# Squares and normalisation on GpSimd, omega scaled once, and block 0's gate work in two pieces

## The chip, the cores and the metric

One core of a Trainium2 chip. The metric is device time in microseconds, the median of three timed runs. The core has five engines that run side by side, each through its own queue in order: PE (TensorE, matrix products), DVE (VectorE), ACT (ScalarE), POOL (GpSimd) and SP, which here issues DMAs. They wait for each other through semaphores.

## The reference

A linear-attention layer with random features, followed by a gated feed-forward layer.

```python
scale = 1.0 / np.sqrt(np.sqrt(D))
def phi(x):                                   # x is q * scale or k * scale
    proj = np.einsum('bhsd,md->bhsm', x, omega)
    sq = np.sum(x * x, axis=-1, keepdims=True) / 2.0
    h = proj - sq
    h = h - np.max(h, axis=-1, keepdims=True)
    return np.exp(h) / np.sqrt(m)
kv = np.einsum('bhsm,bhsd->bhmd', k_p, v)
z = np.sum(k_p, axis=2)
num = np.einsum('bhsm,bhmd->bhsd', q_p, kv)
den = np.einsum('bhsm,bhm->bhs', q_p, z)[..., None] + 1e-06
x = num / den                                 # heads side by side: 4608 x 512
xn = x / np.sqrt(np.mean(x * x, axis=-1, keepdims=True) + 1e-06) * rms_g
g = xn @ w_gate
out = (g * (1.0 / (1.0 + np.exp(-g))) * (xn @ w_val)) @ w_out
```

8 batches of 8 heads, 576 tokens, head size 64, 128 features; 4608 tokens of 512 columns; an inner width of 1536. The weights of the second layer are 64-bit numbers, which the kernel narrows to 32 bits itself.

## The kernel before

The 4608 tokens are 36 chunks of 128, and 9 blocks of 4 chunks (512 tokens). Three stages follow each other on PE.

The first stage (to about 445 us) makes the attention, and a part of the gated layer with it. For each chunk of k and of q, `features` (L457) loads the chunk (`load`, L465), squares it (`square` on ACT, L472), sums the squares by head (`norm` on DVE, L512, or `norm_pe` on PE for the "lean" chunks, which are the first four of k), projects it on omega (`project` on PE, L521, tiles `pjk` and `pjq`), takes the row's largest value (`peak` on DVE, L536), works out the shift (`shift` on DVE, L542: two operations on 128x8, tiles `hm` and `bi`) and takes the exponentials (`exps` on ACT, L552). `kv_mid` and `kv_half` multiply k's features with v. `attend` (L681) then turns q's features around (`turn`, tiles `qt`, `qpT`), multiplies them with kv (`mix`, tile `nu`), divides on DVE (`divide`, L710, tile `x`), and normalises: `power` on ACT (L725) gives the sum of squares `ss`, `root` on POOL (L732) the inverse root, `scale` on DVE (L739) multiplies x by `ss` and by `g_sb` (rms_g on all partitions). `xturn` turns the chunk around on PE (tile `xt`), `xout` and `xhi` on ACT and `xlo` on POOL (L770) write it as a high and a low part, since every product of the gated layer is made of three passes (`three_pass`, L216): high by high, high by low, low by high.

`gated` (L814) makes 4 of the 12 column groups f of the gated layer during this stage: for block `blk` and group f it runs 12 products of 128x512 for the gate (tile `ff`) and 12 for the value, then `gate` on ACT, `silu` and `value` on DVE, and a store. It needs the four chunks of its block (`xs`, L871) and the narrowed weights of its group (`weights`, L315: ACT takes the size, DVE runs four operations, `mag` twice and `w` twice; ACT and POOL write the high and low parts).

The second stage makes the other 8 column groups, and the third the output product, both by a seven-product scheme on halves; neither is touched.

The order of all this is not the order of the code. Every piece of work is an item with an engine, a duration, what it needs, what buffers it takes, and a key (`Plan.add`, L129). `Plan.order` (L133) plays the items through with these durations and, on each engine, starts the ready item with the smallest key; the instructions are then written out in that order, so each engine's queue is fixed. The table `KEYS` (L37) holds the keys of the first nine chunks and of the weights. While PE has nothing ready and no gated item has begun, the player puts `spin` products in PE's queue (L886): 128x512 products whose result nobody uses. `SWITCH` (L109) is what the player adds when PE goes from one form of product to another.

Of the kernel before, what the change touches and what calls it, by code (L numbers as in the profile page):

```python
# [19 lines left out]
DM = H * D  # L20
DFF = 1536
P = 128
# [14 lines left out]
KEYS = {  # L37
    "k": [-34.2, -24.4, -20.3, -13.7, -13.0, -5.6, -2.0, -0.5, -0.4],
    "q": [-32.4, -12.2, -8.0, -2.2, 3.5, 4.9, 5.3, 6.0, 7.6],
    "w": [  # L40
        -9.6, -3.4, 8.7, 11.5, 8.0, 3.2, 4.4, 5.9,
        -16.1, -0.3, -12.6, -18.6, -20.2, -13.8, 26.9, 39.6,
    ],
    "lead": 4.04,
    "v": 3.37,
    "kv": -15.15,
    "attend": -21.79,
}
AHEAD = 28
PACE = (-2, 2, 0, 1.25)  # L50
FIRST = {"k": 1, "q": 0}
# [6 lines left out]
    "mix": {  # L58
        "xr": (2, 1), "xn": (1, 1), "x": (1, 1), "qpT": (1, 1), "kv": (4, 1), "small": (16, 1),
        "mag": (2, 1), "w": (4, 1), "sr": (1, 1), "f64": (2, 1),  # L60
# [47 lines left out]
FRONT = 0.45  # L108
SWITCH = 0.096  # L109
FILL = 900.0  # L110
# [117 lines left out]
def performer_glu_kernel(  # L228
# [69 lines left out]
    nc.scalar.dma_start(om[D:P, :], omT)  # L298
    heads2 = cpool.tile([P, 4], F32, name="heads2")
    cpool.tile([P, 14], F32, name="pad")  # L300
    nc.gpsimd.memset(heads2, 0.0)
    for i in range(2):
        nc.gpsimd.memset(heads2[i * D : (i + 1) * D, i : i + 1], 1.0 / SCALE)
        nc.gpsimd.memset(heads2[i * D : (i + 1) * D, 2 + i : 3 + i], 1.0)

# [151 lines left out]
    def features(tag, c, key):  # L457
# [14 lines left out]
        def square():  # L472
            n = t["raw"][:, 1, :]
            nc.scalar.activation(n, t["raw"][:, 0, :] if lean else n, AF.Square, scale=0.25)

        def norm_pe():
            t["sq"] = tile_("psM", [P, H], f"sq{nm}")
            for hp in range(4):
                nc.tensor.matmul(
                    t["sq"][:, 2 * hp : 2 * hp + 2],  # L480
                    lhsT=t["raw"][:, 1, hp * P : (hp + 1) * P],
                    rhs=heads2[:, 0:2] if first else heads2[:, 2:4],
                    start=True,
                    stop=True,
                )
# [20 lines left out]
        def exp_half(i):  # L506
            if i == 0:
                st[tag + "p", c] = tile_(tag + "p", [P, H, M], f"{tag}p{c}")
            to = st[tag + "p", c].rearrange("p (a b) m -> p b a m", b=2)
            nc.scalar.activation(to[:, i], t["pts"][i], AF.Exp, scale=SCALE)  # L510

# [30 lines left out]
        def shift():  # L542
            hm = small("hm", f"hm{nm}")
            t["bi"] = small("bi", f"bi{nm}")
            ve.scalar_tensor_tensor(
                out=hm, in0=t["mx"], scalar=SCALE, in1=t["sq"], op0=ALU.mult, op1=ALU.subtract
            )
            ve.scalar_tensor_tensor(  # L548
                out=t["bi"], in0=hm, scalar=-1.0, in1=t["sq"], op0=ALU.mult, op1=ALU.subtract
            )  # L550

        def exps(n):  # L552
            if n == 0:
                st[tag + "p", c] = tile_(tag + "p", [P, H, M], f"{tag}p{c}")
            h0 = n // 2 + 4 * (n % 2)
            for h in (h0, h0 + 2):
                nc.scalar.activation(  # L557
                    st[tag + "p", c][:, h, :],
                    t["pts"][h % 2][:, h // 2, :],
                    AF.Exp,  # L560
                    bias=t["bi"][:, h : h + 1],
                    scale=SCALE,
                )
# [117 lines left out]
    def attend(c, key):  # L681
# [43 lines left out]
        def power():  # L725
            t["xn"] = tile_("xn", [P, DM], f"xn{c}")
            t["ss"] = small("ss", f"ss{c}", 1)
            nc.scalar.activation(  # L728
                t["xn"], t["x"].rearrange("p h d -> p (h d)"), AF.Square, accum_out=t["ss"]
            )  # L730
# [8 lines left out]
        def scale():  # L739
            ve.scalar_tensor_tensor(  # L740
                out=t["xn"],
                in0=t["x"].rearrange("p h d -> p (h d)"),
                scalar=t["ss"],
                in1=g_sb,
                op0=ALU.mult,
                op1=ALU.mult,
            )

# [40 lines left out]
        for half in range(2):  # L789
# [23 lines left out]

    def gated(blk, f, key):  # L814
        t = {}

        def ff(j, a=0, z=TB, only=None):
            xhi, xlo = st["xT", blk]
            if a == 0 and not only:
                t[j] = tile_(bank, [P, TB], f"ff{blk}_{f}_{j}")  # L820
            three_pass(
# [10 lines left out]
        def gate():  # L832
            t["t"] = tile_("t", [P, TB], f"t{blk}_{f}")
            nc.scalar.activation(t["t"], t[0], AF.Tanh, scale=0.5)

        def silu():
            t["u"] = tile_("u", [P, TB], f"u{blk}_{f}")
            ve.scalar_tensor_tensor(
# [3 lines left out]
        def value():  # L842
            t["h"] = tile_("h", [P, TB], f"h{blk}_{f}")
            ve.scalar_tensor_tensor(
# [3 lines left out]
        def store():  # L848
            nc.sync.dma_start(h_d[:, f, blk * TB : (blk + 1) * TB], t["h"])
# [5 lines left out]
        at = (blk, f)  # L855
        ws = [[st["w", f, j]] + st.get("ff", []) for j in range(2)]
        give = [("xT", blk)] if f == last else []
        end = blk == NBLK - 1
# [17 lines left out]
        else:  # L876
            g = add("PE", 2.73, lambda: ff(0), xs + ws[0], key, [(bank, at, 0)])
            v = add("PE", 2.73, lambda: ff(1), [g] + ws[1], key, [(bank, at, 1)], give)
        gates.append(v)
        st["ff"] = [v]  # L880
        i = add("ACT", 0.53, gate, [g], top, [("t", at)])
        i = add("DVE", 0.62, silu, [i], top, [("u", at)], [("t", at), (bank, at, 0)])
        i = add("DVE", 0.62, value, [i, v], top, [("h", at)], [("u", at), (bank, at, 1)])
        st["hs", f, blk * TB, TB] = add("SP", 0.26 / RATE, store, [i], top, give=[("h", at)], land=LAND)

# [624 lines left out]
```

## Time and profile before

| | us |
|---|---|
| median of three runs | 1064.76 (1064.54 to 1065.6) |
| span of the profiled execution | 1061.9 |
| busy in it: PE / DVE / ACT / POOL | 1049.1 / 825.5 / 647.7 / 143.8 |
| first gate product starts at | 70.2 |

The profile is of one execution, by the hardware profiler; the span goes from its first to its last instruction, and the page gives no other time of that execution. The runs' times hold what lies around the span as well. A matmul's duration in the trace overlaps the next one's, since they are pipelined, so the pace of PE is read from start to start. "L222" is line 222 of the kernel; a row such as `L474 ACT ACTIVATE inq<-inq ... x36 | 24.8, 695` is a group of 36 instructions with 24.8 us busy in all and 695 ns in the mean; what follows is the engine's idle time before them and who ended it. The granted clock of PE is full throughout.

### The profile page before, as it was taken

The numbers are of one execution on the slowest core, as the hardware profiler recorded it, in microseconds if no ns is written. First come the engines' busy times: TensorE is split into PE (matmuls) and PEld (weight loads), VectorE is DVE, ScalarE is ACT, GpSimd is POOL, SyncE is SP. The second block draws the span as 40 slices with busy tenths as digits, with TensorE's granted clock in tenths as the row PEclk, the third lists the DMA queues.
The fourth block names the chain that finished last, engine by engine and source line by source line (L and its number), as shares of the span: only waits on it lengthen the run. The fifth ranks groups of instructions, "written<-read, shape, count | busy, mean of one in ns | idle before, by whom it ended". The sixth has DMA issues, their size and how long they took to land.

```text
span 1061.9 us, 20636 instructions
## 1 busy us (share of the span) xinstructions
PE 1049.1 (99%) x7755; PEld 881.8 (83%) x7755; DVE 825.5 (78%) x1438; ACT 647.7 (61%) x1428; POOL 143.8 (14%) x185
## 2 busy tenths in 40 slices
PE   9999999999999999999999999999999999999998
PEld 6788888888888888878889788988888888888888
DVE  5989999888887865589889936758649996859573
ACT  7899788868786754556545546535555554444433
POOL 0242221121121221380000324000000000000000
PEclk9999999999999999999999999999999999999999
DMA  7786778566654433776466524434273936172321
GB/s 263 257 267 196 222 246 251 167 212 216 222 178 161 131 134 106 233 245 211 159 188 215 178 81 153 149 104 139 72 266 112 300 131 221 54 217 86 119 91 50
DMA packets 106596, 185.87 MB, mean 175 GB/s; under 512 B 9088, under 2 KB 51456, under 8 KB 106496
## 3 DMA queue, kind: packets, MB, share of 16 engines
q1 hardware_dynamic: 106272, 184.26, 53.7%
q8 instruction: 61, 1.00, 0.4%
q10 hardware_dynamic: 224, 0.30, 0.1%
q14 instruction: 39, 0.32, 0.1%
HBM read 124.49 MB, written 60.03 MB: 174 GB/s over the span
## 4 chain that ended last, share of the span: by engine, by line
PE 82%; DVE 12%; issue 2%; DMA 2%; ACT 1%; SPq 0%; DVEq 0%; ACTq 0%
PE ff L222 6%; PE ff L224 5%; PE ff L223 5%; PE qa L224 5%; PE qa L222 5%; PE qa L223 5%; PE pa L222 4%; PE pa L224 4%; PE pa L223 4%; PE nu L702 3%; PE pjk L527 3%; PE pjq L527 3%; PE kvp L658 3%; PE qt L691 3%; PE qb L224 2%
## 5 line engine op out<-in xcount | busy, mean ns | idle before, releaser
L222 PE MATMUL ff<-xhi,whi 128*128 128x512 f32 (+2 forms) x296 | 120.8, 408 | 0.0
L224 PE MATMUL ff<-xhi,wlo 128*128 128x512 f32 (+2 forms) x296 | 114.5, 387 | 0.0
L223 PE MATMUL ff<-xlo,whi 128*128 128x512 f32 (+2 forms) x296 | 114.4, 387 | 0.0
L557 ACT ACTIVATE qp<-pjq,biq 128x128 f32<-128x128 f32 x288 | 81.4, 404 | 8.8 <-DVE biq L548 5.3
L557 ACT ACTIVATE kp<-pjk,bik 128x128 f32<-128x128 f32 x280 | 78.8, 403 | 9.9 <-DVE rec L716 8.7
L771 POOL TENSOR_TENSOR xlo<-xr,xhi 128x512 fp32r<-128x512 f32 x36 | 47.3, 1314 | 150.7 <-ACT xhi L768 150.7
L1269 DVE TENSOR_TENSOR hb<-hb,hb 128x1024 f32<-128x1024 f32 (+1 forms) x60 | 66.0, 1114 | 0.7
L222 PEld LDWEIGHTS ff<-xhi,whi 128*128 128x128 f32 x296 | 55.6, 188 | 12.0
L224 PEld LDWEIGHTS ff<-xhi,wlo 128*128 128x128 f32 x296 | 55.6, 188 | 11.8
L223 PEld LDWEIGHTS ff<-xlo,whi 128*128 128x128 f32 x296 | 55.8, 188 | 9.0
L1102 ACT COPY m<-pa 128x512 f32<-128x512 f32 (+1 forms) x40 | 21.8, 544 | 67.6 <-PE pa L224 67.5
L1148 ACT ACTIVATE c<-c 128x512 f32<-128x512 f32 (+1 forms) x60 | 34.9, 589 | 44.4 <-DVE c L1109 44.3
L540 DVE TENSOR_REDUCE mxk<-pjk 128x4 f32<-128x512 f32 x72 | 46.8, 683 | 13.6 <-PE pjk L527 13.6
L1109 DVE TENSOR_TENSOR c<-pb,u 128x512 f32<-128x512 f32 (+1 forms) x40 | 25.3, 632 | 38.7 <-PE pb L224 30.5
L540 DVE TENSOR_REDUCE mxq<-pjq 128x4 f32<-128x512 f32 x72 | 47.0, 683 | 2.0 <-PE pjq L527 1.9
L702 PEld LDWEIGHTS nu<-kv,qpT 128*64 128x64 f32 x1152 | 38.5, 137 | 11.3 <-issue 6.2
L702 PE MATMUL nu<-kv,qpT 128*64 128x65 f32 x1152 | 46.3, 226 | 1.0 <-DVE kv L629 1.0
L728 ACT ACTIVATE xn<-x 128x512 f32<-128x512 f32 x36 | 23.1, 643 | 36.0 <-DVE x L718 26.5
L694 ACT COPY qpT<-qt 128x512 f32<-128x512 f32 x72 | 41.0, 607 | 4.3 <-PE qt L691 3.8
L691 PE MATMUL qt<-ident,qp 128*128 128x128 f32 x288 | 41.1, 275 | 1.0 <-DVE x L718 0.9
L1157 DVE TENSOR_TENSOR c<-c,c 128x512 f32<-128x512 f32 (+1 forms) x60 | 40.2, 676 | 1.7
L527 PE MATMUL pjk<-om,ink 64*128 64x128 f32 x576 | 40.8, 282 | 0.5 <-DMA ink<-in_kx_dram 0.5
(209 smaller groups left out, 3134.6 us busy)
## 6 DMA issues: line engine op xcount, KB each, us to landing
hb<-h_scratch SPq DMA_DIRECT2D x48, 512.0 KB, 4.4
inq<-in_qx_dram SPq DMA_DIRECT2D x36, 512.0 KB, 4.2
ink<-in_kx_dram SPq DMA_DIRECT2D x32, 512.0 KB, 4.5
h_scratch<-c SPq DMA_DIRECT2D x64, 256.0 KB, 2.1
Xb<-xn_scratch SPq DMA_DIRECT2D x28, 512.0 KB, 5.0
f<-in_wgv_dram SPq DMA_DIRECT2D x24, 512.0 KB, 5.2
xn_scratch<-xr SPq DMA_DIRECT2D x36, 256.0 KB, 4.5
h_scratch<-h SPq DMA_DIRECT2D x36, 256.0 KB, 2.9
```

The lines of the kernel that those rows point to most:

```text
L222: nc.tensor.matmul(out, lhsT=ah, rhs=bh, start=first, stop=False, skip_group_check=again)
L223: nc.tensor.matmul(out, lhsT=ah, rhs=bl, start=False, stop=False, skip_group_check=again)
L224: nc.tensor.matmul(out, lhsT=al, rhs=bh, start=False, stop=last, skip_group_check=again)
L527: nc.tensor.matmul(t["pts"][i][:, hp, :], lhsT=x[rows, hp, :], rhs=om[rows, :], start=hp == 0 or not first, stop=True, skip_group_check=first,
L540: ve.tensor_reduce(out=by_half[:, i, :], in_=t["pts"][i], axis=AX.X, op=ALU.max)
L557: nc.scalar.activation(st[tag + "p", c][:, h, :], t["pts"][h % 2][:, h // 2, :], AF.Exp, bias=t["bi"][:, h : h + 1], scale=SCALE,)
L691: nc.tensor.transpose(t["pt", half][:, i, :], st["qp", c][:, 4 * half + i, :], ident)
L694: nc.scalar.copy(t["qpT"][:, 4 * half : 4 * half + 4, :], t["pt", half])
L702: nc.tensor.matmul(pt[lo:hi, i, :], lhsT=t["qpT"][:, h, lo:hi], rhs=st["kv", b][:, h, :], start=True, stop=True,)
L771: nc.gpsimd.tensor_tensor(out=st["xT", blk][1][:, :, cs], in0=t["xr"], in1=st["xT", blk][0][:, :, cs].bitcast(F32), op=ALU.subtract,)
L1157: ve.tensor_tensor(out=t[nm], in0=t[src], in1=g[nm], op=ALU.mult)
L1269: ve.tensor_tensor(out=t[nm, g], in0=t[x, g], in1=t[y, g], op=ALU.subtract)
```

## The change

Four things are done.

- `square` of the chunks that are not lean goes from ACT to POOL, as a product of the chunk with itself; the factor 0.25 squared (0.0625) that ACT applied moves into the two operations of `shift`.
- omega is multiplied by the scale once, on DVE, after its load; `shift` and the exponentials then need no scale. `heads2` shrinks to two columns.
- In `attend`, a new `weigh` on POOL multiplies x by `g_sb` without waiting for `ss`, and `scale`, now on POOL too, multiplies the result by `ss`. `power` on ACT writes its squares to a tile of its own, `junk`.
- `gated` takes a first and a last token. Block 0 is done in two pieces of 256 tokens: all four groups for chunks 0 and 1, then all four for chunks 2 and 3. The other blocks are as before.

The keys of the first chunks and of the weights are new, and `SWITCH` is 0.15. The descriptor scratch at the start of the on-chip memory is cut from its default to 1024 bytes a partition. The instructions of every engine stand in a new order in the first stage; the table itself shows nothing of that order, so the diff gives two of its lines.

```diff
 KEYS = {
-    "k": [-34.2, -24.4, -20.3, -13.7, -13.0, -5.6, -2.0, -0.5, -0.4],
+    "k": [-44.08, -30.96, -51.08, -48.87, -23.88, -1.39, 2.61, 0.79, -3.73],
...
+SPANS = (0, 256, 512)
...
-SWITCH = 0.096
+SWITCH = 0.15
...
+    ve.tensor_scalar_mul(om, om, SCALE)
+    heads2 = cpool.tile([P, 2], F32, name="heads2")
...
         def square():
             n = t["raw"][:, 1, :]
-            nc.scalar.activation(n, t["raw"][:, 0, :] if lean else n, AF.Square, scale=0.25)
+            if lean:
+                nc.scalar.activation(n, t["raw"][:, 0, :], AF.Square, scale=0.25)
+            else:
+                nc.gpsimd.tensor_tensor(out=n, in0=n, in1=n, op=ALU.mult)
...
             ve.scalar_tensor_tensor(
-                out=hm, in0=t["mx"], scalar=SCALE, in1=t["sq"], op0=ALU.mult, op1=ALU.subtract
+                out=hm, in0=t["sq"], scalar=-0.0625, in1=t["mx"], op0=ALU.mult, op1=ALU.add
             )
             ve.scalar_tensor_tensor(
-                out=t["bi"], in0=hm, scalar=-1.0, in1=t["sq"], op0=ALU.mult, op1=ALU.subtract
+                out=t["bi"], in0=t["sq"], scalar=-0.0625, in1=hm, op0=ALU.mult, op1=ALU.subtract
             )
...
-        s = add("ACT", 0.54, square, [i], key)
+        s = add("ACT", 0.54, square, [i], key) if lean else add("POOL", 1.36, square, [i], key)
...
+        def weigh():
+            t["xn"] = tile_("xn", [P, DM], f"xn{c}")
+            nc.gpsimd.tensor_tensor(
+                out=t["xn"], in0=t["x"].rearrange("p h d -> p (h d)"), in1=g_sb, op=ALU.mult
+            )
...
         def scale():
-            ve.scalar_tensor_tensor(
-                out=t["xn"],
-                in0=t["x"].rearrange("p h d -> p (h d)"),
-                scalar=t["ss"],
-                in1=g_sb,
-                op0=ALU.mult,
-                op1=ALU.mult,
-            )
+            nc.gpsimd.tensor_scalar_mul(t["xn"], t["xn"], t["ss"])
...
-        i = add("ACT", 0.64, power, nd, key - 0.5, [("xn", c)])
-        i = add("POOL", 0.8, root, [i], key - 5)
-        i = add("DVE", 0.7, scale, [i], key - 0.4, give=[("x", c)])
+        i = add("ACT", 0.64, power, nd, key - 0.5, [("junk", c)], [("junk", c)])
+        j = add("POOL", 1.36, weigh, nd, key - 5, [("xn", c)])
+        add("NONE", 0, lambda: None, [i, j], give=[("x", c)])
+        i = add("POOL", 0.8, root, [i, j], key - 5)
+        i = add("POOL", 0.75, scale, [i], key - 5)
...
-    def gated(blk, f, key):
+    def gated(blk, f, key, begin=0, stop=TB):
         t = {}
+        W = stop - begin
...
-        xs = [st["x", NC * blk + i] for i in range(NC)]
+        xs = [st["x", NC * blk + i] for i in range(begin // P, stop // P)]
...
-    for blk in range(NBLK):
-        for f in sorted(range(FA), key=lambda f: max(KEYS["w"][2 * f : 2 * f + 2])):
+    turn = sorted(range(FA), key=lambda f: max(KEYS["w"][2 * f : 2 * f + 2]))
+    for begin, stop in zip(SPANS, SPANS[1:]):
+        for f in turn:
+            gated(0, f, 1000 + FA * begin / TB + f * (stop - begin) / TB, begin, stop)
+    for blk in range(1, NBLK):
+        for f in turn:
             gated(blk, f, 1000 + blk * FA + f)
...
-    nc = bacc.Bacc("TRN2", target_bir_lowering=False, num_devices=1)
+    nc = bacc.Bacc(
+        "TRN2", target_bir_lowering=False, num_devices=1, dynamic_dma_scratch_size=1024
+    )
```

More of the change, by code (lines that the diff above doesn't have):

```diff
@@ L481, in norm_pe @@
                     lhsT=t["raw"][:, 1, hp * P : (hp + 1) * P],
-                    rhs=heads2[:, 0:2] if first else heads2[:, 2:4],
+                    rhs=heads2,
                     start=True,
@@ L561, in exps @@
                     bias=t["bi"][:, h : h + 1],
-                    scale=SCALE,
                 )
@@ L812, in performer_glu_kernel, with ff @@
     last = max(range(FA), key=lambda f: max(KEYS["w"][2 * f : 2 * f + 2]))
-    def gated(blk, f, key):
+    def gated(blk, f, key, begin=0, stop=TB):
         t = {}
-        def ff(j, a=0, z=TB, only=None):
-            xhi, xlo = st["xT", blk]
+        W = stop - begin
+        def ff(j, a=0, z=W, only=None):
+            xhi, xlo = (x[:, :, begin:stop] for x in st["xT", blk])
             if a == 0 and not only:
-                t[j] = tile_(bank, [P, TB], f"ff{blk}_{f}_{j}")
+                t[j] = tile_(bank, [P, TB], f"ff{blk}_{f}_{j}_{begin}")[:, :W]
             three_pass(
@@ L854, in gated @@
             plan.until = len(plan.items)
-        at = (blk, f)
+        at = (blk, f, begin)
         ws = [[st["w", f, j]] + st.get("ff", []) for j in range(2)]
-        give = [("xT", blk)] if f == last else []
+        give = [("xT", blk)] if f == last and stop == TB else []
         end = blk == NBLK - 1
```

61 lines of the change are left out of this document (33 added, 28 removed), and 2 rows, old and new, of the table KEYS.

## The prediction

> **What bounds the kernel now.** I read the page's head first, then the busy time by stage, then who PE waited for, then the start of the stream.
>
> ```profile
> span 1061.9 us, 20636 instructions
> PE 1049.1 (99%) x7755; PEld 881.8 (83%) x7755; DVE 825.5 (78%) x1438; ACT 647.7 (61%) x1428; POOL 143.8 (14%) x185
> ...
> PEclk9999999999999999999999999999999999999999
> ...
> PE 82%; DVE 12%; issue 2%; DMA 2%; ACT 1%; SPq 0%; DVEq 0%; ACTq 0%
> ```
>
> PE is busy for 99% of the span at full clock, and 82% of the chain that ended last is PE. The profiled span is 1061.9 us and the timed runs have a median of 1064.76, so 2.9 us lie around the span; I add them to every span below.
>
> ```profile
> 445.00:1062.00 617.00, 609.34 (x2945) 512.29 (x2943) 467.35 (x588) 313.50 (x493) 51.43 (x51) 1.00 0.47 154
> 0.00:71.00 71.00, 67.83 (x855) 54.00 (x856) 56.14 (x141) 60.17 (x173) 14.97 (x29) 1.00 0.79 265
> 71.00:126.00 55.00, 53.37 (x640) 45.19 (x640) 51.40 (x121) 49.67 (x140) 15.40 (x19) 1.00 0.64 204
> 126.00:445.00 319.00, 318.56 (x3327) 270.31 (x3324) 250.61 (x591) 224.36 (x624) 61.95 (x87) 1.00 0.60 191
> ```
>
> Each row is a stage: its length, then busy PE, weight loads, DVE, ACT, POOL. From 126 to 445 PE has no gap (318.56 of 319), and DVE and ACT have room. In 71 to 126 DVE is 93% busy and PE loses 1.6 us; that is where three engines are near full. POOL is nearly idle everywhere (92 us of the first 445).
>
> ```profile
> PE pa L222 <- DVE c L1109: 2.9, 4, 1.3
> PE spin L888 <- POOL heads L301: 1.5, 1, 1.5
> PE kvm L619 <- DVE rec L716: 1.0, 1, 1.0
> PE nu L702 <- DVE kv L629: 1.0, 2, 0.5
> ```
>
> Only these waits of PE reach a microsecond. So a faster ACT or DVE gives nothing by itself: the time is the length of PE's stream plus its waits. What can leave the stream is the filler:
>
> ```profile
> L888 PE MATMUL spin<-ones 128*128 128x512 f32 x67 | 23.9, 477 | 1.5 <-POOL heads L301 1.5
> 22.05 2.10 PE spin L888 x7
> 70.21 0.48 PE L222 MATMUL ff<-xhi,whi 128*128 128x512 f32 x1
> ```
>
> 67 spins, 23.9 us, stand in front of the first gate product at 70.21; they do no work of the reference.
>
> **The change, part by part.** *The stream of PE.* In the old order the first gate product follows chunk 4's `nu` and needs all four chunks of block 0:
>
> ```order
> L702 MATMUL nu4_1_1270<-kv1_500,qpT4_1209 64x65
> L888 MATMUL spin_1289<-ones_140 128x512
> L888 MATMUL spin_1293<-ones_140 128x512
> L888 MATMUL spin_1297<-ones_140 128x512
> L691 MATMUL qt5_0_1306<-ident_131,qp5_1219 128x128 x4
> L222 MATMUL ff0_0_0_1314<-xhi0_823,whi0_152 128x512
> L223 MATMUL ff0_0_0_1314<-xlo0_824,whi0_152 128x512
> L224 MATMUL ff0_0_0_1314<-xhi0_823,wlo0_156 128x512
> ```
>
> In the new order it needs chunks 0 and 1 only and follows chunk 3's `nu`:
>
> ```order
> L902 MATMUL spin_1028<-ones_143 128x512
> L708 MATMUL nu3_1_1030<-kv0_525,qpT3_953 64x65 x8
> L220 MATMUL ff0_0_0_0_1048<-xhi0_880,whi0_154 128x256
> L221 MATMUL ff0_0_0_0_1048<-xlo0_881,whi0_154 128x256
> L222 MATMUL ff0_0_0_0_1048<-xhi0_880,wlo0_158 128x256
> ```
>
> What moved: block 0's gate work comes in front of chunk 4, and the spins end with it. The whole order holds 55 spins instead of 67; eleven at the very start are in both. The 12 that go are of the later kind, 2.10/7 = 0.30 us each: **-3.6 us** (by the group's mean, 23.9/67 = 0.357, it would be -4.3). Against it, 96 products of 512 columns become 192 of 256. Their step is read from the starts of matmuls that stand back to back:
>
> ```profile
> 100.15 0.40 PE L224 MATMUL ff<-xhi,wlo 128*128 128x512 f32 x1
> ...
> 102.23 0.39 PE L224 MATMUL ff<-xhi,wlo 128*128 128x512 f32 x1
> ...
> 565.10 0.28 PE L222 MATMUL pa<-Rb11h,lw_0h 128*128 128x256 f32 x1
> ...
> 566.53 0.35 PE L222 MATMUL pa<-Rt2h,lw_4h 128*128 128x256 f32 x1
> ```
>
> Nine steps in 2.08 us are 0.231 each; twelve steps in 1.43 us are 0.119. So 192 x 0.119 - 96 x 0.231 = **+0.7 us**. All other work of PE is the same, only in another order. The stream gets 2.9 us shorter.
>
> *Work that leaves ACT and DVE, and lands on POOL.*
>
> ```profile
> L474 ACT ACTIVATE inq<-inq 128x512 f32<-128x512 f32 x36 | 24.8, 695 | 0.6 <-DMA inq<-in_qx_dram 0.6
> L740 DVE SCALAR_TENSOR_TENSOR xn<-x,ss,g_sb 128x512 f32<-128x512 f32 x36 | 31.3, 869 | 3.5 <-POOL ss L737 3.5
> L771 POOL TENSOR_TENSOR xlo<-xr,xhi 128x512 fp32r<-128x512 f32 x36 | 47.3, 1314 | 150.7 <-ACT xhi L768 150.7
> L737 POOL TENSOR_TENSOR ss<-ss,mhalf 128x1 f32<-128x1 f32 x36 | 21.5, 598 | 3.0
> L734 POOL TENSOR_SCALAR ss<-ss 128x1 f32<-128x1 f32 x36 | 7.3, 204 | 138.0 <-ACT xn L728 137.5
> ```
>
> 68 squares leave ACT (68 x 0.695 = 47 us; the four lean chunks of k keep theirs) and 36 scalings leave DVE (31.3 us). Neither is on PE's path after 126; before it they are cover. On POOL a square and the product with `rmsg` are two-input operations of xlo's shape, 1.31 us: 68 + 36 of them are 137 us. The multiplication by `ss` has no row: it lies between 0.20 (L734, one column) and 1.31 (L771, two inputs); I take the middle, 0.75, 27 us. POOL goes from 92 to 256 us in the first 445: it is no bound on the whole, and its latency per chunk (1.31 + 0.80 + 0.75 after the division, where 0.64 on ACT, 0.80 and 0.87 stood) grows by half a microsecond.
>
> The queue of POOL is another matter. Before, around chunks 0 to 2:
>
> ```order
> L734 TENSOR_SCALAR ss0_740<-ss0_740 128x1
> L737 TENSOR_TENSOR ss0_740<-ss0_740,mhalf_138 128x1
> L771 TENSOR_TENSOR xlo0_824<-xr0_809,xhi0_823 128x4x128
> L734 TENSOR_SCALAR ss1_878<-ss1_878 128x1
> L737 TENSOR_TENSOR ss1_878<-ss1_878,mhalf_138 128x1
> ```
>
> and now, in the same place:
>
> ```order
> L742 TENSOR_TENSOR xn0_755<-x0_696,g_sb_139 128x512
> L748 TENSOR_SCALAR ss0_745<-ss0_745 128x1
> L751 TENSOR_TENSOR ss0_745<-ss0_745,mhalf_141 128x1
> L754 TENSOR_SCALAR xn0_755<-xn0_755,ss0_745 128x512
> L475 TENSOR_TENSOR inq4_694<-inq4_694 128x512
> L475 TENSOR_TENSOR ink6_728<-ink6_728 128x512
> L742 TENSOR_TENSOR xn1_874<-x1_818,g_sb_139 128x512
> L778 TENSOR_TENSOR xlo0_881<-xr0_872,xhi0_880 128x4x128
> ```
>
> What moved: squares, which wait for a load of q or k, now stand in front of `xn1` and `xlo0`; if a load is late, the x of a block waits behind it, and PE's gate product behind that. Between chunk 0's scaling and chunk 8's the new queue holds 13 squares, 9 products, 8 xlo and 5 weight remainders (35 x 1.31 = 46 us) and 9 times `ss` and scaling (9 x 1.55 = 14 us): 60 us.
>
> ```profile
> 37.49 0.42 DVE L718 TENSOR_TENSOR x<-nu,rec 128x256 f32<-128x256 f32 x1
> ...
> 112.02 0.42 DVE L718 TENSOR_TENSOR x<-nu,rec 128x256 f32<-128x256 f32 x1
> ```
>
> From chunk 0's division to chunk 8's took 74.5 us. The new order of PE has 16 spins, 24 projection products and 3.4 us of gate work fewer in between, about 12 us less, so it leaves 62: POOL would be 97% full there.
>
> *DVE against POOL.* Three operations of DVE in the stretch took far longer than their twins, each while a big POOL operation ran:
>
> ```profile
> 45.40 1.27 POOL L771 TENSOR_TENSOR xlo<-xr,xhi 128x512 fp32r<-128x512 f32 x1 [3.63 <-ACT xhi L768]
> 45.55 1.41 DVE L336 TENSOR_SCALAR mag<-mag 128x512 f32<-128x512 f32 x1
> 47.00 0.43 DVE L344 TENSOR_SCALAR mag<-mag 128x512 int32<-128x512 int32 x1
> ...
> 92.40 1.27 POOL L396 TENSOR_TENSOR wlo<-w,whi 128x512 fp32r<-128x512 f32 x1 [6.19 <-ACT whi L393]
> 93.03 0.66 DVE L545 SCALAR_TENSOR_TENSOR hmq<-mxq,sqq 128x8 f32<-128x8 f32 x1
> ...
> 102.06 0.57 DVE L545 SCALAR_TENSOR_TENSOR hmk<-mxk,sqk 128x8 f32<-128x8 f32 x1
> 102.66 0.17 DVE L548 SCALAR_TENSOR_TENSOR bik<-hmk,sqk 128x8 f32<-128x8 f32 x1
> ```
>
> They end where the POOL operation ends, and lost 0.98, 0.49 and 0.40: 1.9 us beside 30.4 us of POOL (0 to 126), 0.06 per us. By chunk 8 the change adds 22 squares, 9 products and 9 scalings, 47 us, so 3 us more are lost. The other end: by then DVE starts 46 such pieces (22 shifts, two pairs for each of 12 weight tiles); if POOL is in the way of 6 in 10, for half of 1.3 us, 18 us are lost. Below nothing it cannot go. I take 4, near the rows. The cover is the nine scalings freed by then, 9 x 0.869 = 7.8 us, less what the new order spends by asking for the same x earlier: I take 5. So 4 is covered, and the waits stay as they are.
>
> [...]
>
> The small edits (omega scaled once on DVE before the first projection, the scale left out of the exponentials, `heads2`, the descriptor scratch) cost nothing: 0.2 us of DVE in the start that it idles through.
>
> **Sum.** 1061.9 - 3.6 + 0.7 = 1059.0 span, 1061.9 us as a run: 0.27% faster. About 0.2% (2.1 us) is what a measurement here tells from no change, so it is just visible.
>
> **The rivals.** *POOL's queue takes the gain back.* At 60 of 62 us any surplus is PE's: with a scaling of 1.31 in place of 0.75 nine chunks cost 5 us more, 3 beyond the room, so 1061.9 + 3 = 1064.9, no change. For it: the 97%; against: squares can run ahead of need, and POOL may have done some before chunk 0. 0.32.
>
> *DVE is held up by POOL and PE waits for it.* Place: the pieces that feed chunks 0 to 8. Up to 5 us of loss is covered; from 7.9 on (5 + 2.9) the kernel is slower than before. At 18 us it is 1061.9 + 13 = 1075; at 12, 1069. For it: DVE is 93% busy there and POOL more than doubles; against: the rate in the rows. 0.23.
>
> *The waits shrink too.* The 1.6 us that PE loses in 71 to 126 are waits for DVE with its scalings in front; without them 1060.3, and with 0.357 a spin and the 2.9 us of `pa` waits gone, 1056.7. 0.12. The forecast itself has 0.33.
>
> **Numbers.** Faster by over 0.2% is the forecast and the shrinking waits, 0.45; same 0.32; slower 0.23. The low end is the 1056.7 just given, rounded down to 1056.5; the high end 1070.5 cuts the second rival beyond 13.6 us of loss, about 0.1.
>
> **What would show it.** In the profile after: 55 spins of some 20 us; first gate product near 56 us instead of 70 (14 us less of the stream stands in front of it: 12 us as counted above, and 2 us of chunk 4's `nu` and spins); PE without gaps from 126 on; DVE operations of 128x8 mostly at 0.17. I am wrong if PE waits for xlo or for DVE's shifts by more than 3 us before 126, if the L754 scaling takes over 1.3 us, or if the stage after 445 changes by more than 3 us, about which nothing here is said.

## The result, and the profile after

| | before | after |
|---|---|---|
| median of four runs (us) | 1065.07 | 1095.74 |
| runs | 1064.54 to 1065.6 | 1095.49 to 1096.5 |
| span of the profiled execution | 1061.9 | 1094.7 |

The changed kernel takes 1.0296 times as long (95% interval 1.0282 to 1.0311): 30.7 us slower, where 2.9 us faster had been forecast, and far above the high end of 1070.5.

The page of the changed kernel, its busy times and the shares of the chain that ended last:

```profile
span 1094.7 us, 20947 instructions
PE 1060.2 (97%) x7839; PEld 894.5 (82%) x7839; DVE 834.8 (76%) x1411; ACT 613.0 (56%) x1364; POOL 321.1 (29%) x323
...
PE 69%; DVE 10%; issue 3%; POOL 2%; ACT 1%; DMA 1%; SPq 0%; DVEq 0%; POOLq 0%; ACTq 0%
```

PE falls from 82% of the chain to 69%, and a POOL that was used for 143.8 us is used for 321.1. The same by stage (length, then busy PE, weight loads, DVE, ACT, POOL, and the granted clock of PE):

```profile
0.00:60.00 60.00, 53.60 (x559) 41.65 (x561) 46.50 (x105) 38.92 (x114) 26.86 (x35) 0.94 0.67 234
60.00:140.00 80.00, 67.75 (x827) 60.73 (x826) 73.31 (x147) 57.11 (x177) 58.64 (x56) 0.95 0.63 195
140.00:480.00 340.00, 329.96 (x3514) 280.10 (x3514) 250.16 (x575) 206.32 (x589) 187.79 (x185) 0.99 0.57 182
480.00:1094.00 614.00, 608.89 (x2944) 512.02 (x2942) 464.86 (x586) 310.62 (x488) 47.80 (x50) 1.00 0.47 154
```

All of the loss is in the first stage: after it PE is busy for 608.89 us where it was 609.34. In the first three rows PE idles for 6.4 + 12.3 + 10.0 = 28.7 us; in the same stage of before it was 5.2. Over the whole span PE idles for 34.5 us where it was 12.8, 21.7 more, and is busy for 11.1 more (1060.2 against 1049.1); together this is the 32.8 by which the spans differ. Most of the busy part stands in the column of the clock. It was 1.00 everywhere, and is now below it: in seven stretches of 3.41 us each PE was granted half its clock. That is 7 x 3.41 / 2 = 11.9 us at most, and 10.4 by the steps of the products that are shown under "The clock". With the stream 2.9 us shorter, 2 to 4 us by which PE's other products take longer are left open.

Who PE waited for:

```profile
PE ff L220 <- DVE u L848: 5.3, 3, 2.5
PE nu L708 <- DVE x L724: 5.1, 2, 2.6
PE xt L759 <- DVE rec L722: 4.6, 3, 2.0
PE kvm L625 <- DVE kv L635: 2.6, 2, 2.1
PE xt L759 <- POOL xn L754: 2.5, 3, 1.5
PE xt L759 <- POOL ink L475: 2.2, 1, 2.2
```

In these six rows 17.6 us are for DVE and 4.7 for POOL. Nothing is spread thin: there are few waits, most of them of 2 us or so. Why DVE is late shows in its rows beside POOL's at one such place:

```profile
65.44 1.28 POOL L394 TENSOR_TENSOR wlo<-w,whi 128x512 fp32r<-128x512 f32 x1
65.46 0.42 DVE L724 TENSOR_TENSOR x<-nu,rec 128x256 f32<-128x256 f32 x1
65.80 0.94 DVE L552 SCALAR_TENSOR_TENSOR hmq<-sqq,mxq 128x8 f32<-128x8 f32 x1
66.68 1.28 POOL L742 TENSOR_TENSOR xn<-x,g_sb 128x512 f32<-128x512 f32 x1
66.78 1.20 DVE L555 SCALAR_TENSOR_TENSOR biq<-sqq,hmq 128x8 f32<-128x8 f32 x1
```

`hmq` ends at 66.74, when POOL's operation ends at 66.72; POOL starts its next one at 66.68, and the second half of the shift is held until that one ends too. Two operations of 0.17 us have become 2.1. The division `x`, whose `nu` lies in PSUM, keeps its 0.42 beside the same POOL operation; all 72 divisions of this run last 0.42 or 0.43. To count this, I take for each operation of DVE what it lasted over the 30th percentile of its kind (the same line and shape), where that is over 0.12 us, below 450 us: 10.5 us in 16 operations in the kernel before, 41.8 us in 63 in the changed one. Of these, 3.6 and 23.4 us lie in the first 150 us. Every one of these operations overlaps an operation of POOL. I call this "lost beside POOL" below.

The groups of POOL that the prediction priced (count, busy time, mean):

```profile
L754 POOL TENSOR_SCALAR xn<-xn,ss 128x512 f32<-128x512 f32 x36 | 59.2, 1645 | 3.5
L742 POOL TENSOR_TENSOR xn<-x,g_sb 128x512 f32<-128x512 f32 x36 | 46.4, 1288 | 76.3 <-DVE x L724 41.7 <-DVE hmq L552 20.3 <-PE xt L759 10.3
L475 POOL TENSOR_TENSOR ink<-ink 128x512 f32<-128x512 f32 x32 | 35.5, 1113 | 25.2 <-DMA ink<-in_kx_dram 25.2
```

The scaling, taken at 0.75 us, lasts 1.65; a square lasts 1.11 and not 1.31.

### The profile page after: what moved, and what is told of

It is laid out like the page before. It is cut to its first block, busy times and chain, and to the rows that moved or that the text cites. A ratio compares the mean times of both kernels' runs of the same rounds, so it can differ in the third digit from the quotient of the medians.

```text
span 1094.7 us, 20947 instructions
## 1 busy us (share of the span) xinstructions
PE 1060.2 (97%) x7839; PEld 894.5 (82%) x7839; DVE 834.8 (76%) x1411; ACT 613.0 (56%) x1364; POOL 321.1 (29%) x323
## 3 DMA queue, kind: packets, MB, share of 16 engines
q8 instruction: 62, 1.02, 0.4%
## 4 chain that ended last, share of the span: by engine, by line
PE 69%; DVE 10%; issue 3%; POOL 2%; ACT 1%; DMA 1%; SPq 0%; DVEq 0%; POOLq 0%; ACTq 0%
PE ff L220 5%; PE qa L222 5%; PE qa L220 5%; PE qa L221 4%; PE pa L220 4%; PE ff L222 4%; PE ff L221 4%; PE pa L221 4%; PE pa L222 4%; PE qb L220 2%; PE qb L222 2%; PE qb L221 2%; PE pb L220 2%; PE pb L221 2%; PE pb L222 2%
## 5 line engine op out<-in xcount | busy, mean ns | idle before, releaser
L220 PE MATMUL ff<-xhi,whi 128*128 128x512 f32 (+3 forms) x328 | 128.9, 393 | 6.0 <-DVE u L848 5.3
L222 PE MATMUL ff<-xhi,wlo 128*128 128x512 f32 (+3 forms) x328 | 122.1, 372 | 0.0
L221 PE MATMUL ff<-xlo,whi 128*128 128x512 f32 (+3 forms) x328 | 121.9, 372 | 0.0
L564 ACT ACTIVATE kp<-pjk,bik 128x128 f32<-128x128 f32 x280 | 79.5, 417 | 28.7 <-DVE bik L555 19.4
L220 PEld LDWEIGHTS ff<-xhi,whi 128*128 128x128 f32 x328 | 63.2, 193 | 17.6 <-DVE u L848 5.9
L222 PEld LDWEIGHTS ff<-xhi,wlo 128*128 128x128 f32 x328 | 63.2, 193 | 10.8
L221 PEld LDWEIGHTS ff<-xlo,whi 128*128 128x128 f32 x328 | 63.5, 194 | 8.3
L742 POOL TENSOR_TENSOR xn<-x,g_sb 128x512 f32<-128x512 f32 x36 | 46.4, 1288 | 76.3 <-DVE x L724 41.7
L1120 ACT COPY m<-pa 128x512 f32<-128x512 f32 (+1 forms) x40 | 21.7, 543 | 70.4 <-PE pa L222 70.3
L754 POOL TENSOR_SCALAR xn<-xn,ss 128x512 f32<-128x512 f32 x36 | 59.2, 1645 | 3.5
L971 POOL TENSOR_TENSOR lw_0l<-wr,lw_0h 128x256 fp32r<-128x256 f32 x8 | 8.5, 1066 | 157.9 <-ACT lw_0h L966 157.9
L733 ACT ACTIVATE junk<-x 128x512 f32<-128x512 f32 x36 | 22.9, 637 | 50.0 <-DVE x L724 50.0
L700 ACT COPY qpT<-qt 128x512 f32<-128x512 f32 x72 | 40.6, 603 | 13.3 <-PE qt L697 13.2
```

The costliest lines, as they stand in the source:

```text
L220: nc.tensor.matmul(out, lhsT=ah, rhs=bh, start=first, stop=False, skip_group_check=again)
L221: nc.tensor.matmul(out, lhsT=ah, rhs=bl, start=False, stop=False, skip_group_check=again)
L222: nc.tensor.matmul(out, lhsT=al, rhs=bh, start=False, stop=last, skip_group_check=again)
L564: nc.scalar.activation(st[tag + "p", c][:, h, :], t["pts"][h % 2][:, h // 2, :], AF.Exp, bias=t["bi"][:, h : h + 1],)
L700: nc.scalar.copy(t["qpT"][:, 4 * half : 4 * half + 4, :], t["pt", half])
L742: nc.gpsimd.tensor_tensor(out=t["xn"], in0=t["x"].rearrange("p h d -> p (h d)"), in1=g_sb, op=ALU.mult)
```

## The experiments

The theories. **Holding**: POOL's operations hold DVE's, DVE is late, PE waits. (Two of the expectations call this a port of POOL's; how POOL holds DVE no run shows, only how long.) **Queue**: the scaling is twice as long as planned and POOL's queue delivers late. **Order**: the new keys and pieces leave too little slack, whatever engine does the work. **Clock**: PE's waits of 2 us cost a second time, through the clock. Unless said otherwise, times are medians, beside the kernel before in the same comparison.

### Undoing one move in the changed kernel

```diff
 scale_act:
-            nc.gpsimd.tensor_scalar_mul(t["xn"], t["xn"], t["ss"])
+            nc.scalar.activation(t["xn"], t["xn"], AF.Copy, scale=t["ss"])
 square_act:
-                nc.gpsimd.tensor_tensor(out=n, in0=n, in1=n, op=ALU.mult)
+                nc.scalar.activation(n, n, AF.Square)
```

> The changed kernel with one operation put elsewhere: the multiplication by ss (1.6 us on POOL, 0.75 in the plan and in the prediction) is done on ACT, in the same place of the order of issue; everything else stands as in the changed kernel. If the mis-sized scaling and the POOL queue behind it made the loss (POOL loses 58 us of work; by chunk 8 some 9 x 0.85 = 8 us that the plan did not know), the waits of PE for xn and the clock drops behind them go: 1070 to 1080 us. If it is DVE being held by POOL's two-input operations, little changes: in the trace of the changed kernel only 3.7 of 43 us that DVE operations lose below 450 us lie beside a scaling, so 1088 to 1096.

Measured: 1089.5 us (ratio 1.0235, 1.022 to 1.025); 43.3 us lost beside POOL.

> The changed kernel with the 68 squares done on ACT again, in the same place of the order of issue. If POOL's two-input operations hold DVE up, DVE gets back the 18 us that it loses beside squares (11 to 14 of them before chunk 8) and PE's waits before 140 us mostly go, with the clock drops behind them: 1070 to 1080 us, and DVE's 128x8 operations fall back to 0.17. If the scaling of 1.6 us in POOL's queue made the loss, it stays at that duration and the time is 1085 to 1095. If neither engine is the matter but the order itself, 1090 to 1098.

Measured: 1085.2 us (1.0191, 1.0176 to 1.0206); 30.5 us lost.

> Both of the last two: squares and scaling on ACT, the product with g_sb (36 x 1.3 us) still on POOL, order of issue as in the changed kernel. If the two moves to POOL made the loss by either road: 1062 to 1070 us with no or one clock drop. If the new order has too little slack whatever engine does the work: above 1080.

Measured: 1085.8 us (1.0206, 1.0189 to 1.0223); 24.1 us lost, one stretch at half clock.

Each move that is undone gives something back, the squares most (10.5 us), but the two together give 10 and not 25 to 30. Neither the holding nor the queue as I had them explains that. In the last run the waits have moved to ACT, which does 104 operations more at places that were planned without them:

```profile
PE pjq L528 <- ACT qp L564: 3.2, 5, 1.1
PE qt L697 <- ACT xr L765: 2.6, 3, 1.2
PE xt L759 <- DVE x L724: 2.5, 2, 1.3
```

So these runs mix the moves with an order made for other engines. From here on each kernel is planned anew.

### The order without the moves, and the moves without the order

> The changed kernel without the moves to POOL: its new keys, block 0 in two pieces, omega scaled once and SWITCH 0.15, but squares on ACT and the scaling as one operation on DVE, as before, and the order planned anew with those engines (64 spins in it, 67 before, 55 in the changed kernel). If the moves to POOL made the loss, DVE's operations lose some 9 us instead of 43, no clock drop is left after the start, and the time is 1062 to 1067 us. If the new keys and pieces themselves leave too little slack, it stays above 1080.

Measured: 1083.0 us (1.0175, 1.016 to 1.019), above the 1080 that was named for an order with too little slack; 15.0 us lost beside POOL.

> As the last one, but with the keys and SWITCH of the kernel before as well, so that only the pieces of block 0 and omega scaled once are left of the change (56 spins). The part of the prediction on the stream says 11 spins less, 3.3 us, and 0.7 us for the smaller products: 1062 us if the waits stay, 1065 or more if PE then waits instead of spinning.

Measured: 1079.0 us (1.014, 1.0123 to 1.0157); 8.7 us lost, two stretches at half clock.

This was in none of my rivals: without a single operation moved to POOL, the pieces of block 0, and the new order that comes with them, cost 14 us. The stream did what the prediction said, 56 spins and the first gate product at 55.6 us instead of 70.2. Then PE waits:

```profile
PE xt L764 <- DVE xn L752: 5.5, 3, 2.8
PE qt L700 <- DVE x L727: 5.1, 5, 1.9
```

These are waits for DVE's division and scaling, the long ones all between 70 and 126 us, where DVE was 93% busy before (51.40 of 55) and is 91% busy here (50.03). The eleven spins that were taken out are only 3.3 us. More is missing in PE's queue at that place, which shows in the gate products (`ff`) from 71 to 126 us, first before, then in this run (length, then busy PE):

```profile
71.00:126.00 55.00, 23.09 (x94) 1.00 0.64 204
```

```profile
71.00:126.00 55.00, 6.74 (x48) 0.97 0.67 211
```

Before, all of block 0's gate and value products stand up to 126 us, 96 of 512 columns, between the products of chunks 4 to 8. Here only 84 of its 192 products of 256 columns do, and the next follow at 130.5 us. As I read it, this work, with the spins, had covered the time until DVE was done. Why the player put it later is not shown.

> The changed kernel with the true durations of the two POOL operations in the planner (scaling 1.62 instead of 0.75, square 1.09 instead of 1.36), the order planned anew (61 spins). If the loss came from the order being made for a scaling of 0.75, PE's waits for xn and for DVE before 140 us shrink to less than half: 1068 to 1078 us. If DVE being held by POOL made it, which no duration in the planner tells, 1085 to 1096.

Measured: 1105.0 us (1.0388, 1.0354 to 1.0422). Telling the planner the true durations does not win the loss back but makes it worse; an order made for a scaling of 0.75 us is not the whole cause.

> The changed kernel with the keys and SWITCH of the kernel before and all moves to POOL (55 spins): what the moves do without the new keys. If POOL makes the loss, by its port or its queue, about as slow as the changed kernel, 1085 to 1105 us. If the keys made it, 1062 to 1070.

Measured: 1099.8 us (1.033, 1.0315 to 1.0345); 52.5 us lost. The moves add 20.8 us to the 1079.0 of the same keys, and the new keys win some 4 of these back.

> The changed kernel with the keys and SWITCH of the kernel before and block 0 in one piece: the moves to POOL, and omega scaled once, alone (67 spins, as before). With pieces and old keys the moves made 1079 into 1100. If their cost is the holding of DVE by POOL whatever the order, 1064 + 20 = 1080 to 1090 us. If moves and pieces only hurt together, because the pieces ask for more of DVE before 126, 1065 to 1072.

```diff
-SPANS = (0, 256, 512)
+SPANS = (0, 512)
```

Measured: 1086.3 us (1.0195, 1.0177 to 1.0213); 50.7 us lost. That is 15.3 more than the next run, which has none of the moves: with block 0 whole they cost somewhat less than the 20.8 beside the pieces.

> The kernel before with omega scaled once, the smaller heads2 and the cut descriptor scratch, and nothing else (67 spins). If the 14 us of the run with old keys and pieces come from the pieces, this is 1063 to 1066 us; if they come from omega's scaling, the new form of the shift or the scratch, it is near 1079.

Measured: 1071.0 us (1.0052, 1.0035 to 1.0069), between the two expectations. `junk` and the planner's slightly different durations for the gate items are in it too, and the order differs in places. Up to 126 us this run goes as the kernel before (first gate product at 70.3 us, PE idle for 4.6 us against 4.8). Near 430 us PE waits 2.4 us for a chunk's high and low parts, and 6.8 us at half clock follow.

> The kernel before with SWITCH 0.15 in place of 0.096 and nothing else: the same instructions, planned into another order (74 spins, 7 more, 2 us). It shows what another order costs by itself. If the order of before is no better than its neighbours, 1065 to 1068 us; if any new order loses to it what the run with omega alone lost and more, 1070 to 1080, and part of the 14 us of pieces and old keys is that and not the pieces.

Measured: 1071.3 us (1.0064, 1.0049 to 1.008). The same instructions in another order lose 7.3 us, of which 2 are spins. Hardly any of it is waiting: PE idles for 1.0 us more than before and is busy for 6.2 more, and why its products take longer in this order is open. So two orders other than that of before, with no piece and no move in them, lost some 5 us each, the one late and by the clock, the other in its products. If the order of the run with old keys cost as much by itself, 8 to 9 of its 14 us are left for the pieces; that it did is not shown.

### The moves apart

> Of the moves to POOL only the squares: old keys, block 0 in one piece, omega scaled once, the scaling one operation on DVE, planned anew with 1.09 us for a square (63 spins). To be read beside the moves together (1086.3) and none of them (1071.0). The holding of DVE puts the cost here: POOL's products with two inputs, 71 us of them, at the 0.24 us lost per us; 1079 to 1086. If the chain through the scaling on POOL costs most, 1069 to 1075.

Measured: 1083.4 us (1.018, 1.0161 to 1.02), 14.1 more than the run with omega alone, each beside its own runs of the kernel before; 43.8 us lost beside POOL against 8.2 there.

> Of the moves only the product with g_sb and the scaling (1.3 and 1.6 us per chunk on POOL), with squares on ACT; otherwise as the last one (81 spins). POOL's queue, and the chain from the division to the turned chunk with it, puts the cost here: 1079 to 1086. If it is the holding of DVE, half of the moves' two-input work is left out and DVE is freed of 31 us: 1069 to 1076. The 14 spins more than before are 4 us of filler in either case.

Measured: 1080.5 us (1.0156, 1.0138 to 1.0174), 11.2 more in the same way, of which 4 are planned filler; 30.8 us lost, no half clock.

Without the filler the squares cost twice as much as the scaling, as the holding would have it. The 30.8 us lost here cost only 7: beside this stands DVE freed of 31 us.

### POOL work that nobody waits for, in the kernel before

What does POOL's work cost by itself? After each `xlo` the kernel before gets idle operations on a tile of its own, in three forms; the descriptor scratch is cut to make room.

```diff
                 op=ALU.subtract,
             )
+            for _ in range(3):   # load_read
+                nc.gpsimd.tensor_tensor(out=idle[1], in0=idle[0], in1=idle[0], op=ALU.mult)
+            for _ in range(3):   # load_write; 6 in load_write6
+                nc.gpsimd.memset(idle[1], 1.0)
+            for _ in range(2):   # load_one
+                nc.gpsimd.tensor_scalar_mul(idle[1], idle[0], mhalf)
```

> The kernel before, with three more POOL operations after each xlo: products of an idle 128x512 tile with itself (about 1.05 us each by the squares of the changed kernel, 108 of them, 113 us), whose result nobody waits for. The order of every other engine is the one of before; of POOL's own work only what stands behind them is late, by up to 3.2 us. If two-input operations on POOL hold DVE up, DVE's operations lose some 113 x 0.2 = 23 us more below 450 us than the 9 of before, and PE waits for DVE before 126: 1068 to 1080 us. If POOL's queue alone matters, DVE's durations stay, and PE waits for what POOL makes (xlo, ss): 1065 to 1075.

> The same with three memsets of a 128x512 tile in place of the products: an operation of POOL that reads nothing and only writes. If DVE is held by what POOL reads through a port of both (two inputs above all: in the changed kernel DVE lost 0.24 us per us of squares and 0.06 per us of the one-input scaling), DVE's losses stay near the 9 us of before; if any POOL operation holds it, they grow as in the run with products, per us of POOL. By POOL's queue the time grows with the memsets' own duration, which no run has shown: 1064 to 1075 us.

> The kernel before with six memsets of an idle 128x512 tile after each xlo (0.53 us each by the run with three, so 3.2 us, as long as the three products of 1.10 of the run with reads, 3.3): the same time in POOL's queue, without a read. If the 26 us that the products cost came from the queue (DVE's scaling waited 6.1 us for ss there before 150, 2.2 with three memsets), this run costs as much, 1085 to 1092 us. If they came from POOL reading while DVE reads, it costs little more than three memsets, 1067 to 1073, and DVE's operations lose some 12 us below 450, not 44.

> The same with two multiplications of an idle tile by a column of one number per partition (the operation of the new scaling, one tile read, 1.6 us each: 3.2 us per chunk, as much time in the queue as the products). If one-input operations hold DVE as the products do, 1085 to 1092 us and DVE loses over 30 us; by the trace of the changed kernel (0.06 us lost per us of scaling against 0.24 of squares) DVE loses some 9 + 115 x 0.06 = 16 us and the time is that of the six memsets plus at most 5.

| run | POOL added (us) | lost beside POOL (us) | time | ratio (95%) |
|---|---|---|---|---|
| before | 0 | 10.5 | 1063.7 to 1065.7 | 1 |
| load_write | 57.6 | 13.2 | 1068.7 | 1.0043 (1.003 to 1.0056) |
| load_write6 | 115.5 | 13.9 | 1081.1 | 1.0144 (1.0128 to 1.016) |
| load_one | 118.3 | 18.6 | 1078.9 | 1.0128 (1.011 to 1.0146) |
| load_read | 119.2 | 44.4 | 1091.4 | 1.0259 (1.0237 to 1.0282) |

The two halves of q's shift on DVE in the kernel before:

```profile
L545 DVE SCALAR_TENSOR_TENSOR hmq<-mxq,sqq 128x8 f32<-128x8 f32 x36 | 8.2, 227 | 1.0
L548 DVE SCALAR_TENSOR_TENSOR biq<-hmq,sqq 128x8 f32<-128x8 f32 x36 | 6.0, 167 | 1.2
```

The group on POOL and the same two halves, with the products:

```profile
L778 POOL TENSOR_TENSOR idle<-idle 128x512 f32<-128x512 f32 x108 | 119.2, 1104 | 5.6
...
L545 DVE SCALAR_TENSOR_TENSOR hmq<-mxq,sqq 128x8 f32<-128x8 f32 x36 | 12.9, 357 | 1.0
L548 DVE SCALAR_TENSOR_TENSOR biq<-hmq,sqq 128x8 f32<-128x8 f32 x36 | 11.6, 321 | 1.2
```

with the memsets:

```profile
L778 POOL MEMSET idle<- 128x512 f32 x216 | 115.5, 535 | 10.4
...
L545 DVE SCALAR_TENSOR_TENSOR hmq<-mxq,sqq 128x8 f32<-128x8 f32 x36 | 7.7, 213 | 1.0
L548 DVE SCALAR_TENSOR_TENSOR biq<-hmq,sqq 128x8 f32<-128x8 f32 x36 | 6.0, 167 | 1.2
```

and with the one-input multiplications:

```profile
L778 POOL TENSOR_SCALAR idle<-idle,mhalf 128x512 f32<-128x512 f32 x72 | 118.3, 1642 | 3.4
...
L545 DVE SCALAR_TENSOR_TENSOR hmq<-mxq,sqq 128x8 f32<-128x8 f32 x36 | 8.4, 232 | 1.0
L548 DVE SCALAR_TENSOR_TENSOR biq<-hmq,sqq 128x8 f32<-128x8 f32 x36 | 7.7, 214 | 1.2
```

The three fill POOL's queue for the same time, and DVE is held by the products above all. Over the 10.5 us of before, (44.4 - 10.5) / 119.2 = 0.28 us are lost per us of them, 8.1 / 118.3 = 0.07 of one-input multiplications, 3.4 / 115.5 = 0.03 of memsets. Yet memsets and multiplications cost 13 to 15 us too. That is the queue: DVE's scaling waits for `ss`, which now stands behind them. The wait over the span, before, with the memsets, with the multiplications, and with the products:

```profile
DVE xn L740 <- POOL ss L737: 3.5, 4, 1.1
```

```profile
DVE xn L740 <- POOL ss L737: 22.4, 15, 2.8
```

```profile
DVE xn L740 <- POOL ss L737: 18.6, 14, 2.4
```

```profile
DVE xn L740 <- POOL ss L737: 12.8, 13, 2.4
```

So both theories hold in the kernel before, each with a price of its own: some 3.2 us more in POOL's queue per chunk costs 13 to 15 us, and that the same time is spent reading two inputs costs 12 to 14 more (27.7 us over its own runs of before, against 15.4 and 13.3). With three memsets, 1.6 us per chunk, it was 5. With the products DVE is late itself, so that it waits less for `ss`. The clock has its share in these prices: 13.7 us at half clock with the six memsets and with the products, 6.8 with the multiplications and none with three memsets, worth up to half as much.

### The clock

```diff
             t["xt"] = tile_("psM", [P, NCC, P], f"xt{c}")
+            for _ in range(6 if c in (3, 5, 8, 26, 30) else 0):
+                nc.tensor.matmul(
+                    t["xt"].rearrange("p a b -> p (a b)"),
+                    lhsT=ones[:, :P], rhs=ones, start=True, stop=True,
+                )
```

> The changed kernel with 30 filler products of 128x512 more (six, some 1.8 us, ahead of the turning of chunks 3, 5, 8, 26 and 30, which stand at five of PE's stalls of over 2 us); nothing is taken away. If the drops of the granted clock to half, 2 to 4 us after such stalls and 3.4 us long, are a cost of their own, these five go, each worth 1.7 us: 1095.7 - 8.5 = 1087 us, with the waits for DVE and POOL as long as before counted with the filler. If the drops come from something else than PE's idling, they stay and the time is 1096 or, with the filler on the path, up to 1105.

Measured: 1096.2 us (1.0292, 1.0276 to 1.0307), no faster than the changed kernel, although the time at half clock fell from 23.9 to 10.2 us, which is worth up to 6.8. Half of this fall is not the filler's: the drops at 12.1 and 36.0 us in the changed kernel lie ahead of the first filler and are missing in this profile, though PE stands still for the same 2.14 us near 35 us in both. Of the five places the drops at three are gone; those near 338 and 389 us came again, the last one twice as long. At the first of the places the filler did not stand in the wait but behind it:

```profile
72.36 1.16 PE L528 MATMUL pjq<-om,inq 64*128 64x128 f32 x16
75.59 1.68 PE L759 MATMUL xt<-ones 128*128 128x512 f32 x6 [2.08 <-ACT qpT L700]
77.11 0.60 PE L764 MATMUL xt<-ident,xn 128*128 128x128 f32 x4
```

It waits for the buffer of `xt` first, 2.08 us (2.17 in the changed kernel), and then adds its own time. This run therefore does not show what the clock alone costs. What the drops cost is read from the trace of the changed kernel itself. The same gate products, first at full clock, then within a drop:

```profile
63.59 0.28 PE L221 MATMUL ff<-xlo,whi 128*128 128x256 f32 x1
...
64.79 0.28 PE L222 MATMUL ff<-xhi,wlo 128*128 128x256 f32 x1
```

```profile
76.47 0.65 PE L759 MATMUL xt<-ident,xn 128*128 128x128 f32 x4 [2.17 <-POOL ink L475]
...
77.36 0.42 PE L222 MATMUL ff<-xhi,wlo 128*128 128x256 f32 x1
...
79.28 0.41 PE L222 MATMUL ff<-xhi,wlo 128*128 128x256 f32 x1
```

Ten steps in 1.20 us are 0.120 each; nine in 1.92 are 0.213. So 0.093 of each 0.213 us is lost within a drop, 10.4 of the 23.9 us.

## Why the prediction was wrong, by its steps

**The stream.** Right as far as it was counted: 55 spins, steps of 0.120 us for 256 columns, and the part after the first stage unchanged within 2 us. That the rest of PE's work only changes its order, at no cost, was not: its products take 2 to 4 us longer in all than the spins, the pieces and the clock account for. The first gate product was wanted near 56 us and came at 63.4 in the changed kernel, but at 55.6 with the old keys.

**"The waits stay as they are"** is the sentence that failed, in three ways.

*It took the spins for time that could be had, and the early gate work for free.* The prediction's own rows said who was full there: DVE, 51.40 of 55 us busy from 71 to 126. In the run without any move PE was early and then waited, and 14 us were lost. The spins alone (3.3 us) cannot be all of this; in that run the gate products that had stood between PE's waits for DVE no longer stand there (6.74 us of them from 71 to 126, where there were 23.09). For asking for the same x earlier the prediction took 2.8 us (7.8 less 5). How much of the 14 us any other order would have cost is not shown; two that kept their spins lost 5. In the changed kernel itself 19.03 us of gate products stand from 71 to 126, so how far this holds there, beside the moves, is open. No rival had this: all took the 1.6 us that PE lost up to 126 as a property of the work, and it was one of the order.

*The holding of DVE was mis-sized.* The holding itself and its place were right, and it was the second rival. The rate of 0.06 us per us came from three rows, of a time when POOL was 24% busy and when its work seldom met a shift. The whole first stage of the kernel before has three times that: DVE lost 8.7 us beside the 47.3 us of `xlo`, 0.18 per us. Measured for two-input work: 0.21 in the changed kernel, 0.28 in the run with idle products. Up to 134 us, when chunk 8 has been turned around, DVE lost 22.6 us where it lost 2.6 before: 20 more, where 4 was taken and 18 was the upper end. That end had 28 pieces caught for 0.65 us each; it was 32 operations, for 0.71. It counted a pair once, and the rows above show both halves caught.

*POOL's queue and its chain.* The scaling, between 0.20 and 1.31, was taken at 0.75; it is 1.65, outside both ends. From a chunk's last division to its scaled `xn` it took 3.6 us on average over chunks 0 to 8 before and 5.2 after; half a microsecond was forecast. PE waits 4.7 us for POOL itself, and putting the scaling back on ACT gave 6.3. The first rival priced this at 3 us. It feared 60 us of POOL's work in 62 us from chunk 0's division to chunk 8's; it became 60.8 in 76.3, since the stretch itself grew. So the queue is not full on the whole (58.64 of 80 us in the window from 60), but it is in places: from 56.6 to 76.4 us POOL has no pause over 0.2 us, and what stands at its end comes late. The loads that it feared ahead of `xn` hold it little there: of the 25.2 us that POOL waits for `ink`, 5.0 lie between 44 and 140 us.

**The clock** was in no step. Six of its seven drops come with a stop of PE of 2.0 us or more, within 1.2 us of its end; the first, at 12.1 us, does not. They cost 10.4 to 11.9 us of the 32.8.

**The signs that were named.** Two signs of being wrong bear on this: the scaling over 1.3 us, which is there, and PE waiting by over 3 us for `xlo` or for DVE's shifts before 126. That one is there only in effect: PE waits for what stands behind the shifts in DVE's queue (`x`, `kv`, `rec`, `u`) and for POOL's `xn`, hardly for the shifts and not for `xlo`. PE was to have no gap from 126 on and idles for 10 us between 140 and 480. The shifts of 128x8 were to stay mostly at 0.17:

```profile
L552 DVE SCALAR_TENSOR_TENSOR hmq<-sqq,mxq 128x8 f32<-128x8 f32 x36 | 14.8, 410 | 0.9
L555 DVE SCALAR_TENSOR_TENSOR bik<-sqk,hmk 128x8 f32<-128x8 f32 x32 | 9.9, 310 | 1.1
```

They take 0.41 and 0.31 on average.

The sum as measured: pieces and another order 14.0, the moves 20.8 on top of that, the new keys -4, together 30.8. It must come to the 30.7 of the change, since each run differs from the last by one step; it tells where the loss appears, not why. Within the moves, squares and scaling cost 14.1 and 11.2 alone and 15.3 together (all against omega alone), so they do not add, and how the holding, the queue and the clock share these 15 to 21 us in the changed kernel itself is open; the idle loads show only that holding and queue each can cost 10 us and more. Also open is why the keys of the changed kernel help the moves and hurt without them.

No version here beats the kernel before.

## What to carry to other kernels

Filler in the queue of the engine that is the bound is time only if nothing else is late there: before counting it as won, look who is nearly full in the same stretch. Here that was DVE, busy for 51.40 of 55 us; 3.3 us of spins were taken out in the run with old keys, and 14 us were lost. The same may hold for real work that stands between waits: moved elsewhere, it no longer covers them. Work moved to an idle engine is priced by what it holds up and by what stands behind it in that engine's queue; 177 us of "free" POOL time cost 15 to 21 us here. And an order that was found for one set of durations is a part of the kernel: change anything in its plan, and time the new order with nothing else changed.

## What the runs showed of the hardware

What held DVE up was above all two-input work of POOL: beside the idle products 0.28 us of DVE's time were lost per us of POOL's, beside memsets, which read nothing, 0.03. Beside the one-input multiplication, which reads as well, it was only 0.07. In the changed kernel all 63 of DVE's operations that were held overlap an operation of POOL, and they lost 41.8 us. What in the chip makes DVE wait is not shown.

PE's granted clock fell to half for 3.41 us at a time (two such times in a row in places, as in the 6.8 us near 430 us with omega alone), mostly at waits of about 2 us. In the changed kernel each of the six stops of PE of 2.0 us or more (2.03 to 2.63) had a drop begin within 1.2 us of its end, and none of the five of 0.95 to 1.8 us (0.98 to 1.76) had one; the drop at 12.1 us stands by no stop. In the 19 profiles of this study PE stood still for 2.0 us or more 35 times, and in 28 of these a drop began during the stop or within 4.5 us of its end; of 30 stops of 1.5 to 2.0 us it was 7, and of 69 stops of 0.95 to 1.5 us (without the first wait of each program) 10. So in these runs such a wait made a drop likely and not certain: the same stop of 2.14 us near 35 us was followed by one in the changed kernel and by none in the run with filler.
